# Batch 0's v is loaded beside k instead of behind q, and the first stage of a fused attention and MLP kernel is put in a new order

## The chip, the core and the metric

One Trainium2 chip, one of its cores. The metric is the device time of one execution, in microseconds (us), as the median of several runs. The engines are named as in the profile: PE (TensorE, with PEld for its weight loads), DVE (VectorE), ACT (ScalarE), POOL (GpSimd) and SP (SyncE). SP, ACT and POOL also issue DMAs; the transfers that SP issues show in the profile as queue q1, those that POOL issues as q0, those of ACT as q10.

## What is computed

```python
# per batch (8) and head (8): q, k, v are 576 x 64
q_s = exp(q - q.max(-1)) / sum over the 64 features
k_s = exp(k - k.max(tokens)) / sum over the 576 tokens
kv  = k_s^T v                              # 64 x 64 per head
x   = q_s kv, heads side by side           # 576 x 512 per batch
xn  = (x - mean) / sqrt(var + 1e-6) * g    # over the 512 columns
out = x + relu(xn w1) w2                   # w1: 512 x 2048, w2: 2048 x 512
```

Inputs and the output are fp32. The kernel multiplies in bf16.

## The kernel before

**Work as a whole.** Tokens 0 to 511 of a batch are one piece of work: four tiles of 128 tokens. The last 64 tokens of all eight batches make a ninth piece. For each piece the kernel forms x, normalises it, and runs the two MLP products on PE. The MLP products fill PE from about 15 us to the end. `run(main, side)` interleaves the two kinds of work by hand: `main` is the list of MLP steps, each with a weight, and `side` is a list of (position, function) that are issued when the running sum of the weights has reached the position. So the order on every engine is fixed when the kernel is built (`manual_schedule`), and each engine works through its list in order.

**Batch 0 is special.** Nothing can hide its attention, so `first_batch` writes that part out instruction by instruction. Its 576 tokens of k and v lie in 96 partitions with six tokens each (`T0 = 6`), in four pairs of heads (j = 0 to 3).

The loads are issued in this order. SP: q of tiles 0 and 1 (`load_q0(0, 2, nc.sync)`), then k in four pieces, one per head pair. ACT: the rows of g, 2 KB. POOL: first a small copy into a tile called `gate` (L1004), which reads a piece of q's tile; since POOL works in order, everything behind it waits until q's tiles 0 and 1 have landed. Behind it POOL issues v in three pieces (heads 0 to 3, 4 and 5, 6 and 7; L1006), q of tiles 2 and 3 (L970), the first 512 columns of w1 in two halves (L1013; by rows 0 to 255 and 256 to 511), the other three blocks of w1 (L99), and then w2 and the next batches.

The computation of batch 0 then goes like this:

- `exp_qt(0, t)` (ACT, L220) and `norm_q` (DVE: L229, L274, L923) make tile t of the softmax of q; `eq_pT` transposes it on PE (L928) and copies it to SBUF (L934 on DVE, L930 on ACT).
- `exp_k0(j)` (ACT, L293) is exp of k for head pair j. `z0_mm(j)` (PE, L306, 6 matmuls with one column) sums it over the tokens. `recip_z` (DVE, L314) inverts the sums, once for all four pairs. `kv0_mm(j)` multiplies exp(k) by v (PE, L321, 6 matmuls), scales the result on DVE (L322) into `kv_sb`, and spreads its negative row mean into `mbc` (L327 on ACT for j < 3, L331 on DVE for j = 3).
- `xT_mm(j, kh)` (PE, L342) forms, for tiles 0 and 1 and half kh of the columns, x transposed and with its mean already taken off. All four j add into one bank, so the bank is complete only after j = 3. `xT_out(i)` (L351 on DVE for i = 0 and 1, L353 on ACT for i = 2 and 3) scales column block i by g and writes it to `xnT`, the operand of the first MLP product.
- Tiles 2 and 3 go another way, inside the MLP steps: `q0_rest(t)` (PE: `zs` L940 and `po` L414), `x_fast` and `x_normed` (DVE: L464, L475), then `xn_pT` (PE L928, DVE L932).
- `warm(n)` issues n matmuls (L867) on a tile of zeros whose result nobody reads.

**The first MLP product** of batch 0 is `ph` (PE, L520). Its first eight matmuls need `xnT` of i = 0 and 1 and the first half of the first w1 columns; the next eight need i = 2 and 3 and the second half. After these come the matmuls for tile 2, then those that use the second block of w1 columns, and so on.

Of the kernel before, what the change touches and what calls it, by code (L numbers as in the profile page):

```python
# [12 lines left out]
FP32 = mybir.dt.float32  # L13
BF16 = mybir.dt.bfloat16
AF = mybir.ActivationFunctionType
# [5 lines left out]
def kernel(  # L21
# [16 lines left out]
    nc = tc.nc  # L38
# [4 lines left out]
    P = 128  # L43
# [3 lines left out]
    KO1 = DM // P  # L47
    KO2 = DH // P
    NP = H // 2
# [6 lines left out]
    T0 = 6  # L56
    P0 = S // T0
# [16 lines left out]
    gate = const.tile([P, 4], FP32)  # L74
# [42 lines left out]
    raws = {}  # L117
# [99 lines left out]
    def exp_qt(b, t):  # L217
        if t == 0 and b:
            new_eq(b)
        nc.scalar.activation(eqs[b][0][:, t], raws[b][2][:, :, t], AF.Exp)  # L220
# [68 lines left out]
    def exp_k0(j):  # L289
        hs = slice(2 * j, 2 * j + 2)  # L290
        if j == 0:
            eks[0] = raw.tile([P, T0, H, D], BF16, tag="kt", name="ek0", bufs=1)
        nc.scalar.activation(  # L293
            eks[0][0:P0, :, hs, :].rearrange("p t h d -> p h t d"), raws[0][0][0:P0, hs], AF.Exp
        )

    def k0_mm(j, t):
        hs = slice(2 * j, 2 * j + 2)
        return eks[0][0:P0, t, hs, :], raws["v0"][0:P0, hs, t, :], P

    def z0_mm(j):

        if j == 0:
            kvbox["z0"] = mm_ps.tile([P, NP], FP32, tag="m", name="z0")
        for t in range(T0):
            nc.tensor.matmul(  # L306
                kvbox["z0"][:, j : j + 1], k0_mm(j, t)[0], ones[0:P0],
                start=(j == 0 and t == 0), stop=(t == T0 - 1), skip_group_check=True,
            )

    def recip_z():
        kvbox["rz"] = sml.tile([P, NP], FP32, tag="rzk", name="rzk")
        kvbox["sum"] = sml.tile([P, NP], FP32, tag="lnv", name="kvs")
        nc.vector.reciprocal(kvbox["rz"], kvbox["z0"])  # L314

    def kv0_mm(j):
        pool, tag = (att_ps, "a") if j < 2 else (mm_ps, "m")
        pkv = pool.tile([P, P], FP32, tag=tag, name="pkv")
        for t in range(T0):
            lhsT, rhs, w = k0_mm(j, t)  # L320
            nc.tensor.matmul(pkv[:, 0:w], lhsT, rhs, start=(t == 0), stop=(t == T0 - 1))  # L321
        nc.vector.scalar_tensor_tensor(  # L322
            kv_sb[:, 0, j, :], in0=pkv, scalar=kvbox["rz"][:, j : j + 1], in1=diag,
            op0=ALU.mult, op1=ALU.mult, accum_out=kvbox["sum"][:, j : j + 1],
        )
        if j < NP - 1:
            nc.scalar.activation(  # L327
                mbc[:, j], ones_w, AF.Copy, scale=kvbox["sum"][:, j : j + 1]
            )
        else:  # L330
            nc.vector.tensor_scalar_mul(  # L331
                out=mbc[:, j], in0=ones_w, scalar1=kvbox["sum"][:, j : j + 1]
            )

    def xT_mm(j, kh):

        if j == 0:
            pobox["T", kh] = mm_ps.tile([P, 2, 2, P], FP32, tag="m", name="pxT")
        ops = [(kv_sb[:, 0, j, :], j % 2)] if j // 2 == kh else []
        ops += [(mbc[:, j], i) for i in range(2)]  # L340
        for n, (lhsT, i) in enumerate(ops):
            nc.tensor.matmul(  # L342
                pobox["T", kh][:, i], lhsT, eqTs[0][:, 0:2, j, :],
                start=(j == 0 and n == 0), stop=(j == NP - 1 and n >= len(ops) - 2),
                skip_group_check=True,
            )

    def xT_out(i):
        dst, src = xnTs[0][:, 0:2, i, :], pobox["T", i // 2][:, i % 2]
        if i < 2:  # L350
            nc.vector.tensor_scalar_mul(out=dst, in0=src, scalar1=g_one[:, i : i + 1])  # L351
        else:
            nc.scalar.activation(dst, src, AF.Copy, scale=g_one[:, i : i + 1])  # L353
# [509 lines left out]
    def warm(n):  # L863

        w = mm_ps.tile([P, 4, P], FP32, tag="m", name="warm")
        for _ in range(n):
            nc.tensor.matmul(w, junk, junk[:, 0:4].to_broadcast([P, 4, P]), start=True, stop=True)  # L867
# [77 lines left out]
    def eq_pT(c, t, eng):  # L945
        pe_T(eqTs[c], eqs[c][0][:, t].rearrange("p h d -> p (h d)"), t, eng)
# [4 lines left out]
    def g_columns():  # L951
        gcp = mm_ps.tile([P, KO1], FP32, tag="m", name="gcp")
        nc.tensor.matmul(gcp, raws["g"], ident_f, start=True, stop=True)
        nc.vector.tensor_copy(out=g_one, in_=gcp)
        nc.vector.tensor_scalar_mul(out=g_col, in0=gcp, scalar1=1.0 / DM)

    def first_batch():

        nc.scalar.preload_act_table_set("natural_log_exp_and_others")
        raws[0] = (  # L960
            mlp.tile([P, H, T0, D], FP32, tag="hT", name="kt0", bufs=1), None,
            raw.tile([P, H, T, D], FP32, tag="qt", name="qt"),
        )
        k0, _, q0 = raws[0]
        v0 = mlp.tile([P, H, T0, D], BF16, tag="hs", name="v0", bufs=1)
        raws["v0"] = v0

        def load_q0(t, tn, eng):
            ts = slice(t, t + tn)
            eng.dma_start(  # L970
                q0[:, :, ts],
                q[0, :, 0:SM, :].rearrange("h (p t) d -> p h t d", t=T)[:, :, ts],
            )

        def src0(x, h0, hn):
            return x[0, h0 : h0 + hn].rearrange("h (p t) d -> p h (t d)", t=T0)

        load_q0(0, 2, nc.sync)
        for h0 in range(0, H, 2):
            nc.sync.dma_start(  # L980
                k0[0:P0, h0 : h0 + 2].rearrange("p h t d -> p h (t d)"), src0(k, h0, 2)
            )
        raws["g"] = outp.tile([KO1, P], FP32, tag="ot", name="g_rows")
        nc.scalar.dma_start(
            raws["g"], bass.AP(moe_g_ln.tensor, moe_g_ln.offset, [[P, KO1], [1, P]])
        )
        nc.vector.memset(junk, 0.0)
        nc.vector.memset(eps_ln, 1e-6)
        nc.vector.memset(ones, 1.0)
        nc.vector.memset(bones, 0.0)  # L990
        nc.vector.memset(bones[0:64, 0:1], 1.0)
        nc.vector.memset(bones[64:P, 1:2], 1.0)
        nc.vector.memset(ones_w, -1.0 / DM)
        nc.vector.memset(diag, 0.0)
        for ps in halves:
            nc.vector.memset(diag[ps, ps], 1.0)
        nc.vector.memset(kv_sb[:, 1:B], 0.0)
        nc.vector.memset(vr, 0.0)
        for half in range(2):
            nc.vector.memset(vr[64 * half : 64 * half + 64, :, 4 * half : 4 * half + 4, D:], 1.0)  # L1000
        nc.vector.memset(vm[:, :, :, :, D:], 1.0)
        make_identity(nc, ident)
        nc.gpsimd.tensor_copy(out=ident_f, in_=ident[0:KO1, 0:KO1])
        nc.gpsimd.tensor_copy(out=gate, in_=q0[:, 1, 0, 0:4])  # L1004
        for h0, hn in ((0, 4), (4, 2), (6, 2)):
            nc.gpsimd.dma_start(  # L1006
                v0[0:P0, h0 : h0 + hn].rearrange("p h t d -> p h (t d)"), src0(v, h0, hn)
            )
        for t in range(2, T):
            load_q0(t, 1, nc.gpsimd)  # L1010
        for kh in range(2):
            ks = slice(2 * kh, 2 * kh + 2)
            nc.gpsimd.dma_start(w1_sb[:, ks, 0:512], w1_src[:, ks, 0:512])  # L1013
        for nb in range(1, 4):
            load_w1(nb)
        load_w2(0)
        load_w2(1)

        new_eq(0)
        start_x(0)  # L1020
        warm(17)
        for t in range(2):
            exp_qt(0, t)
            norm_q(0, t)
        eq_pT(0, 0, nc.vector)
        warm(6)
        eq_pT(0, 1, nc.vector)
        for j in range(NP):
            exp_k0(j)
            z0_mm(j)  # L1030
            if j == NP - 2:
                g_columns()
        recip_z()
        kv0_mm(0)
        kv0_mm(1)
        kv0_mm(2)
        xT_mm(0, 0)
        kv0_mm(3)
        exp_qt(0, 2)
        exp_qt(0, 3)  # L1040
        xT_mm(1, 0)
        xT_mm(2, 0)
        xT_mm(0, 1)
        xT_mm(3, 0)
        xT_out(0)
        xT_out(1)
        eq_pT(0, 2, nc.scalar)
        xT_mm(1, 1)
        xT_mm(2, 1)
        eq_pT(0, 3, nc.vector)  # L1050
        xT_mm(3, 1)
        xT_out(2)
        xT_out(3)

    def q0_rest(t):
        z_q(0, t)
        for i in range(NP):
            po_mm(0, t, i)
# [33 lines left out]
    with tc.manual_schedule(  # L1092
# [11 lines left out]
        def po_x(c, t):  # L1104
            for i in range(NP):
# [4 lines left out]
            mlp_steps(0),  # L1110
            [
                (2, lambda: (q0_rest(2), x_fast(0, 2), x_normed(2))),
                (4, lambda: q0_rest(3)),
                (6, lambda: (xn_pT(0, 2, nc.vector), x_fast(0, 3), x_normed(3))),
                (8, lambda: [po_mm(0, t, i) for t in range(2) for i in range(NP)]),
                (12, lambda: xn_pT(0, 3, nc.vector)),
# [74 lines left out]
```

## Time and profile before

| what | value |
|---|---|
| median of 3 runs | 262.32 us (262.25 to 262.44) |
| profiled execution, its own time | 262.09 us |
| its span (first to last instruction) | 260.3 us |
| granted PE clock over the span | 1.00 |
| busy: PE, DVE, ACT, POOL | 98%, 86%, 68%, 40% |
| time until PE's first `ph` matmul | 14.62 us |
| PE busy in the stretch 65 to 258 us | 191.26 of 193.00 us |

A row of the timeline reads: start, length, engine, line, operation, what it writes and what it reads, shape, number of instructions, and in brackets the idle time before it with what ended the wait. A row of the chain reads: start, length, what ran. In the rows of a DMA queue the numbers are packets, megabytes (as written at the destination) and the busy share of 16 engines, which passes 100% where packets overlap.

### The profile page before, as it was taken

The page shows a single profiled execution, that of the slowest core. Times are in us where ns is not written, and L with a number is a line of the kernel's source. Part 1 is how long each engine was busy: PE and PEld are TensorE (multiplying, and loading weights), DVE is VectorE, ACT ScalarE, POOL GpSimd, SP SyncE. Part 2 cuts the span into 40 slices and gives each one's busy share as a digit, 9 for nine tenths or more (in the row PEclk, how much of TensorE's full clock was granted, in tenths as well). Part 3 has the DMA queues.
Part 4 walks back from the last instruction along what each step waited for, and adds up shares of the span by engine and source line. Part 5 has one row for each costly group of instructions (what it writes and reads, how often), then busy time and mean ns, then how long its engine had stood idle before and what let it go on. Part 6 is the DMA issues. An engine that isn't in the chain of part 4 may idle for free.

```text
span 260.3 us, 7286 instructions
## 1 busy us (share of the span) xinstructions
PE 253.9 (98%) x2885; PEld 215.6 (83%) x2885; DVE 223.1 (86%) x542; ACT 177.5 (68%) x348; POOL 103.2 (40%) x160
## 2 busy tenths in 40 slices
PE   8899999999999999999999999999999999999993
PEld 3689755788888888888888988888889888888883
DVE  6768996989989998899889988998899889957873
ACT  4747790997988685888588858885788386647400
POOL 3953247410299409800980098008200900190000
PEclk9999999999999999999999999999999999999999
DMA  6999999988699995999699859989902630422014
GB/s 198 257 203 208 354 221 332 257 169 308 118 122 321 268 120 107 300 247 107 142 300 235 86 135 304 232 89 161 279 0 50 142 137 1 77 71 99 3 40 121
DMA packets 82618, 45.04 MB, mean 173 GB/s; under 512 B 58196, under 2 KB 79192, under 8 KB 82584
## 3 DMA queue, kind: packets, MB, share of 16 engines
q0 software_dynamic: 32464, 21.76, 45.8%
q1 hardware_dynamic: 49488, 22.29, 36.8%
q10 hardware_dynamic: 632, 0.53, 0.7%
q8 instruction: 22, 0.36, 0.6%
q14 instruction: 12, 0.10, 0.1%
HBM read 36.70 MB, written 9.44 MB: 177 GB/s over the span
## 4 chain that ended last, share of the span: by engine, by line
PE 92%; DMA 4%; POOL 2%; DVE 0%; issue 0%
PE ba L604 21%; PE bx L762 20%; PE bb L762 10%; PE ph L520 8%; PE bb L604 6%; PE be L604 5%; PE bc L604 5%; PE pc L556 5%; PE bc L762 5%; DMA w_raw<-in_moe_w_ch_dram 3%; PE pkv L371 2%; DMA qt<-in_q_dram 2%; PE po L403 2%; PE ptr L928 1%; PE po L414 1%; POOL v L1006 1%
## 5 line engine op out<-in xcount | busy, mean ns | idle before, releaser
L604 PEld LDWEIGHTS <-hs 128*128 128x128 bf16 x512 | 49.6, 98 | 6.0
L269 POOL TENSOR_TENSOR tq<-xnT 128x256 bf16<-128x256 bf16 x30 | 20.1, 671 | 85.3 <-PE bc L604 73.9
L762 PEld LDWEIGHTS <-w_raw 128*128 128x128 bf16 x480 | 46.7, 98 | 5.5
L604 PEld LDWEIGHTS <-hT 128*128 128x128 bf16 x392 | 37.6, 98 | 4.2
L762 PEld LDWEIGHTS <-w1g 128*128 128x128 bf16 x360 | 34.7, 98 | 4.3 <-issue 0.2
L762 PE MATMUL bx<-tq,w_raw 128*128 128x256 bf16 x240 | 31.3, 273 | 0.0
L604 PE MATMUL ba<-w_q,hs 128*128 128x256 bf16 x256 | 30.6, 273 | 0.0
L786 ACT COPY bc<-bx 128x512 f32<-128x512 f32 x30 | 16.7, 596 | 19.1 <-PE bx L762 19.1
L427 ACT ACTIVATE scrap<-x,mv 128x512 bf16<-128x512 bf16 x32 | 23.1, 723 | 4.6 <-DVE mv L457 4.4
L793 DVE TENSOR_TENSOR bb<-bx,s 128x512 f32<-128x512 f32 x30 | 19.5, 694 | 7.2 <-ACT s L790 4.5
L804 ACT ACTIVATE hT<-bb 128x512 bf16<-128x512 f32 x30 | 16.3, 595 | 9.3 <-PE bb L762 9.3
L804 ACT ACTIVATE hT<-bc 128x512 bf16<-128x512 f32 x30 | 16.5, 595 | 8.5 <-PE bc L762 8.5
L796 DVE TENSOR_TENSOR hT<-bx,s 128x512 bf16<-128x512 f32 x30 | 19.3, 684 | 3.2 <-PE bx L762 3.1
L587 DVE TENSOR_TENSOR hs<-hT 128x1024 bf16<-128x1024 bf16 x32 | 21.4, 672 | 0.5 <-ACT hT L804 0.5
L229 DVE TENSOR_REDUCE zq<-eq 128x16 f32<-128x1024 bf16 (+1 forms) x20 | 20.7, 1049 | 0.5 <-ACT eq L220 0.5
L269 POOL TENSOR_TENSOR tq<-xnT,tq 128x256 bf16<-128x256 bf16 x30 | 20.0, 669 | 1.1
L449 DVE SCALAR_TENSOR_TENSOR x<-po,rq 128x256 bf16<-128x256 f32 x48 | 17.5, 420 | 1.7 <-PE po L403 1.7
L790 ACT COPY s<-bb 128x512 f32<-128x512 f32 x30 | 16.6, 622 | 0.0
L804 ACT ACTIVATE hT<-bx 128x512 bf16<-128x512 f32 x30 | 16.4, 610 | 0.0
L762 PE MATMUL bx<-xnT,w1g 128*128 128x256 bf16 x120 | 16.2, 273 | 0.0
L762 PE MATMUL bx<-tq,w1g 128*128 128x256 bf16 x120 | 15.9, 272 | 0.0
L762 PE MATMUL bc<-xnT,w1g 128*128 128x256 bf16 x120 | 15.8, 273 | 0.0
(157 smaller groups left out, 535.0 us busy)
## 6 DMA issues: line engine op xcount, KB each, us to landing
out_dram<-ot POOLq DMA_DIRECT2D x30, 256.0 KB, 4.4
kt<-in_k_dram SPq DMA_DIRECT2D x5, 1024.0 KB, 11.6
qt<-in_q_dram SPq DMA_DIRECT2D x4, 1024.0 KB, 9.9
qt<-in_q_dram POOLq DMA_DIRECT2D x2, 1024.0 KB, 12.7
kt<-in_k_dram POOLq DMA_DIRECT2D x2, 1024.0 KB, 14.5
vm<-in_v_dram POOLq DMA_DIRECT2D x16, 128.0 KB, 12.4
qt<-in_q_dram SPq DMA_DIRECT2D x3, 512.0 KB, 5.7
w_raw<-in_moe_w_ch_dram POOLq DMA_DIRECT2D x3, 512.0 KB, 10.5
```

Source lines behind the costliest of these rows:

```text
L229: nc.vector.reduce_sum(eqs[c][1][:, ts], eqs[c][0][:, ts], axis=AX.X)
L269: nc.gpsimd.tensor_tensor(out=dst[:, t], in0=x[:, t], in1=y[:, t], op=ALU.subtract)
L427: nc.scalar.activation(scrap, x[:, t], AF.Square, bias=mv[:, t, 0:1], scale=-float(DM), accum_out=mv[:, t, 1:2],)
L449: nc.vector.scalar_tensor_tensor(x[:, t].rearrange("p (i two d) -> p i two d", two=2, d=D)[:, :, half], in0=pobox[c, t][half], scalar=1.0, ...
L520: nc.tensor.matmul(ph[:, m % 2, at : at + tn], (w1g if c else w1_sb)[:, ko, m * P : (m + 1) * P], xnTs[c][:, t0 : t0 + tn, ko, :], start=( ...
L587: nc.vector.tensor_tensor(out=dst, in0=x, in1=y, op=op)
L604: nc.tensor.matmul(hbox[bank][:, t, cs], lhsT, rhs[:, cs], start=first and (own or t == 0) and k == 0, stop=k == KH - 1, skip_group_check= ...
L762: nc.tensor.matmul(dst[:, q], lhsT, rhs, start=first and q == 0 and ko == 0, stop=ko == 1, skip_group_check=True)
L786: nc.scalar.copy(at[g, "c"], at[g, "x"])
L793: nc.vector.tensor_tensor(out=at[g, "b"], in0=at[g, "x"], in1=at[g, "s"], op=ALU.add)
L796: nc.vector.tensor_tensor(out=h_out(g, 1, 1), in0=at[g, "x"], in1=at[g, "s"], op=ALU.add)
L804: nc.scalar.activation(h_out(g, odd, half), at[g, name], AF.Relu)
```

## The change

- `gate` is now copied from the rows of g (L1005 of the changed kernel), so v and all that POOL issues behind it wait for these 2 KB and no longer for q's tiles 0 and 1.
- `z0`, its inversion and the scaling are set by halves: `recip_z(0)` for pairs 0 and 1, `recip_z(1)` for 2 and 3, with a bank of two columns each. `kv0_mm` keeps the matmuls; the scaling is a step of its own, `kv0_out(j, eng)`, with `mbc` on DVE for j = 0 and 3 and on ACT for j = 1 and 2.
- The written-out order becomes: pairs 0 and 1 up to their `kv0_mm`, the transposes of q's tile 1, g's columns, then pair 2 and pair 3, with `xT_mm` of a pair for both halves kh one behind the other.
- `xT_out` goes to DVE for i = 0 and 2 and to ACT for i = 1 and 3. In the built program ACT's step for i = 1 carries a semaphore wait for DVE's step for i = 0, and that for i = 3 one for i = 2.
- ACT's exp for tiles 2 and 3 stands between these; tile 2's transposes stand at the end of `first_batch`, now copied by DVE; those of tile 3 stand at position 3 of the MLP steps, copied by ACT, and `q0_rest(3)` moves from position 4 to 5.
- The six `warm` matmuls in the middle become three groups of two at other places.

```diff
     def z0_mm(j):
-        if j == 0:
-            kvbox["z0"] = mm_ps.tile([P, NP], FP32, tag="m", name="z0")
+        half, at = divmod(j, 2)
+        if at == 0:
+            kvbox["z0", half] = mm_ps.tile([P, 2], FP32, tag="m", name="z0")
...
-    def recip_z():
+    def recip_z(half):
+        if half == 0:
+            kvbox["rz"] = sml.tile([P, NP], FP32, tag="rzk", name="rzk")
+            kvbox["sum"] = sml.tile([P, NP], FP32, tag="lnv", name="kvs")
+        nc.vector.reciprocal(kvbox["rz"][:, 2 * half : 2 * half + 2], kvbox["z0", half])
...
+    def kv0_out(j, eng):
         nc.vector.scalar_tensor_tensor(
-            kv_sb[:, 0, j, :], in0=pkv, scalar=kvbox["rz"][:, j : j + 1], in1=diag,
+            kv_sb[:, 0, j, :], in0=kvbox["kv0", j], scalar=kvbox["rz"][:, j : j + 1], in1=diag,
             op0=ALU.mult, op1=ALU.mult, accum_out=kvbox["sum"][:, j : j + 1],
         )
-        if j < NP - 1:
+        total = kvbox["sum"][:, j : j + 1]
+        if eng is nc.scalar:
             nc.scalar.activation(mbc[:, j], ones_w, AF.Copy, scale=total)
         else:
             nc.vector.tensor_scalar_mul(out=mbc[:, j], in0=ones_w, scalar1=total)
...
     def xT_out(i):
-        if i < 2:
+        if i % 2 == 0:
             nc.vector.tensor_scalar_mul(out=dst, in0=src, scalar1=g_one[:, i : i + 1])
...
-        nc.gpsimd.tensor_copy(out=gate, in_=q0[:, 1, 0, 0:4])
+        nc.gpsimd.tensor_copy(out=gate[0:KO1], in_=raws["g"][:, 0:4])
...
         eq_pT(0, 0, nc.vector)
-        warm(6)
-        eq_pT(0, 1, nc.vector)
-        for j in range(NP):
+        for j in range(2):
             exp_k0(j)
             z0_mm(j)
-            if j == NP - 2:
-                g_columns()
-        recip_z()
-        kv0_mm(0)
-        kv0_mm(1)
+        recip_z(0)
+        warm(2)
+        for j in range(2):
+            kv0_mm(j)
+        eq_pT(0, 1, nc.vector)
+        g_columns()
+        kv0_out(0, nc.vector)
+        exp_k0(2)
+        z0_mm(2)
+        exp_k0(3)
+        kv0_out(1, nc.scalar)
+        warm(2)
         kv0_mm(2)
         xT_mm(0, 0)
+        xT_mm(0, 1)
+        z0_mm(3)
+        recip_z(1)
         kv0_mm(3)
+        kv0_out(2, nc.scalar)
+        kv0_out(3, nc.vector)
+        xT_mm(1, 0)
+        xT_mm(1, 1)
         exp_qt(0, 2)
-        exp_qt(0, 3)
-        xT_mm(1, 0)
         xT_mm(2, 0)
-        xT_mm(0, 1)
         xT_mm(3, 0)
         xT_out(0)
         xT_out(1)
-        eq_pT(0, 2, nc.scalar)
-        xT_mm(1, 1)
         xT_mm(2, 1)
-        eq_pT(0, 3, nc.vector)
         xT_mm(3, 1)
+        exp_qt(0, 3)
         xT_out(2)
         xT_out(3)
+        eq_pT(0, 2, nc.vector)
+        warm(2)
...
                 (2, lambda: (q0_rest(2), x_fast(0, 2), x_normed(2))),
-                (4, lambda: q0_rest(3)),
+                (3, lambda: eq_pT(0, 3, nc.scalar)),
+                (5, lambda: q0_rest(3)),
```

## The prediction

> **What bounds the kernel now.** I read the page's chain first, to see which engine carries the end.
>
> ```profile
> PE 92%; DMA 4%; POOL 2%; DVE 0%; issue 0%
> ```
>
> PE carries it; DMA and POOL come in only at the start. So I asked for the chain up to 22 us:
>
> ```profile
> 0.74 4.29 DMA qt<-in_q_dram
> ...
> 5.08 0.19 POOL gate L1004
> 5.27 2.07 POOL v L1006 x3
> ...
> 9.82 6.86 DMA w_raw<-in_moe_w_ch_dram
> 16.68 0.05 issue
> 16.72 0.61 PE ph L520 x4
> ```
>
> Up to 16.68 us the chain is loads in one line: q lands, POOL passes its gate, issues v and w1, and the second half of w1's first columns lands at 16.68. After 16.72 PE has no wait of a tenth of a us or more except one near 19.3 us (0.11, on DVE's xn). So whatever moves the second-column block of `ph` (it starts at 19.57) moves the end by as much. Later loads leave room: the next w1 block lands at 10.53 + 8.7 = 19.2 us.
>
> The timeline shows the stage that the change rewrites:
>
> ```profile
> 7.13 0.84 ACT L293 ACTIVATE ek<-kt 96x768 bf16<-96x768 f32 x1 [0.20 <-DMA kt<-in_k_dram]
> 8.16 1.82 ACT L293 ACTIVATE ek<-kt 96x768 bf16<-96x768 f32 x2 [0.19 <-DMA kt<-in_k_dram]
> ...
> 10.22 1.26 PE L321 MATMUL pkv<-v,ek 96*128 96x128 bf16 x18
> ...
> 14.62 0.60 PE L520 MATMUL ph<-xnT,w_raw 128*128 128x256 bf16 x4
> ...
> 16.72 0.61 PE L520 MATMUL ph<-xnT,w_raw 128*128 128x256 bf16 x4 [0.41 <-DMA w_raw<-in_moe_w_ch_dram]
> ```
>
> exp of k follows k's landings one by one (about 7.1, 8.1, 9.1 us). v's first piece, issued at 5.20 and 5.0 us under way, lands at 10.2, and PE's first `pkv` starts there, 4.40 us before the first `ph`. PE then still waits for w1: the first stage has 0.41 us to spare.
>
> The DMA queues in two windows, 5.0 to 7.5 and 7.5 to 8.4 us:
>
> ```profile
> q1 hardware_dynamic: 509, 0.72, 107.7%
> ```
>
> ```profile
> q0 software_dynamic: 117, 0.09, 64.1%
> q1 hardware_dynamic: 98, 0.13, 55.3%
> ```
>
> k alone keeps the engines full. v's packets begin at 7.5, 2.3 us after their issue, as k runs out, and the two share the time. There is no idle DMA time after 2.7 us that an earlier v could fill.
>
> **The change, part by part.** *Gate.* g's 2 KB are moved by 2.1 us (q10's eight packets all lie in the window 1.5 to 2.7). POOL's copy took 0.19, so v is issued near 2.2 instead of 5.20. With v's own delay of 2.3 us its packets begin at about 4.5; with that of an output store on an idle queue (issued 128.41, first packet 129.6: 1.2 us) at 3.4; if they wait for k to run out, at 7.5. I take 4.5, v's own row, and keep both ends. All POOL issues behind v come earlier too, but w1's bytes stand behind the same bytes of q, k and v. With the engines full, w1's landings stay (16.7, 19.2), and so do those of q's tiles 2 and 3 (12.4 and 13.2, where ACT's exps of them start); ACT asks for them at 13.8 and later. What is queued behind the new waits: on ACT, which works in order, a late exp of k holds back the other exps and `mbc`; on PE, `z0` of a late pair holds back all that stands behind it.
>
> *What v takes from k.* k costs 0.72 MB / 1536 B = 470 packets in 2.5 us, 5.3 ns each. v costs 3.8 ns (window 8.4 to 11.0: 698 packets, nearly all v, in 2.6 us). In turns of one packet each, a piece of k (192 packets) takes 192 x 9.1 ns = 1.75 us instead of 1.02. From 4.5 us on, k's pieces then land at 6.5, 8.3, 10.0 and 11.3 (before 6.1, 7.1, 8.1, 9.1) and v's at 8.6, 10.3 and 11.7 (before 10.2, 10.9, 11.7). The Trainium skill (DMA: Bandwidth & Descriptors, "Issuing engines are not separate DMA queues") says that DMAs started by different engines run on the same 16 DMA engines and interleave, so that issuing from several saves only sequencer time. It speaks against this change, and the two windows agree. By it the sum stays as it is; only a rate above both rows would alter it.
>
> *The order behind the first `pkv`.* Let X be the start of the first `pkv`. Before, X = 10.22 and the first `ph` is at X + 4.40. In the new order PE has, from X: two `kv0_mm` 0.67 (12 x 0.056), tile 1's transposes 0.22, g's columns 0.30, `z0_mm(2)` 0.15, two warm matmuls 0.43, `kv0_mm(2)` 0.33, five `xT_mm` matmuls 0.55 with 0.07 of waiting for `mbc`: X + 2.73. Then the last pair's chain: `z0_mm(3)` and its latency 0.32, reciprocal 0.04 + 0.18, scalings of pairs 2 and 3 0.04 + 0.34 + 0.36, `mbc` 0.04 + 0.25, two `xT_mm` to their end 0.45: X + 4.75. DVE's eviction 0.04 + 0.48 and then ACT's, which waits for it, 0.04 + 0.47: X + 5.8. PE meanwhile runs six `xT_mm` (0.65), tile 2's transposes and two warm matmuls (0.65), and reaches the first `ph` at X + 5.9. The stage is 1.5 us longer from X, because the transposes of tile 1, g's columns, half of z0 and four warm matmuls, which stood in the wait for v before, now stand behind it; and the two evictions of a bank are one behind the other (0.99 us; before, 0.88 for two on DVE). The gate has to bring X forward by 1.5 us, to 8.7, only to break even.
>
> *X itself.* X is the later of v's first landing + 0.06, and the second piece of k + 0.04 + 0.84 (exp) + 0.06 + 0.15 (z0) + 0.43 (warm). With the landings above: 8.6 and 8.3 + 1.52 = 9.8. First `ph`: 15.7.
>
> *From the first `ph` to the block that started at 19.57.* Before: 4.95 us, with 0.41 of waiting for w1 in it. New: w1 is there (PE asks for its second half at 17.1), but tile 3's transposes (0.22) stand there, and `zs` of tile 3 then waits about 0.4 for ACT's copy (0.57). DVE's chain for tile 3 (L943, L932, L464, L475) starts later by that too. It adds to 4.98.
>
> *Sum.* 15.7 + 4.98 - 19.57 = +1.1. On the profiled execution's own 262.09 (260.3 of span and 1.8 around it) that is 263.2; the median of the runs stands 0.23 higher, so 263.4. As the bounds of v's start and of the shared rates lean to a smaller cost (v starting at 5.2 gives X = 9.3 and +0.6), I forecast 263.3. Nothing else costs: the reciprocal in two parts adds one 0.18 on DVE while it waits for PE, and `mbc` of pair 0 on DVE 0.25 instead of 0.40.
>
> **Rivals.** *v still starts only when k runs out* (7.5 us), so the load does not move. For: no q0 packet before 7.5, though issued at 5.2. Against: an output store needs only 1.2 us. Then X = 10.24 and `ph` at 16.1: +1.5, 263.8. Chance 0.18.
>
> *v starts at 3.4, while q's tiles are still moving.* q then lands near 5.5 instead of 5.0, k's second piece at 9.1, X = 10.6: +1.9, 264.2. Against: 0.79 MB moved from 2.7 to 5.0, so q is nearly through by then. Chance 0.13.
>
> *Not slower: k and v together move faster than either alone.* For: k ran at 289 GB/s in 5.0 to 7.5 while the queue moved 343 from 2.7 to 5.0. k's second piece at 7.2, v's first at 8.6 and w1 0.7 us earlier need one us saved before 8.7. This decides: with X at 8.63, its floor by exp of k's second piece, `ph` comes at 14.53 and the kernel gains 0.06: 262.3. Earlier v gains nothing more. Against: in 7.5 to 8.4 the shares of both sum to the usual 119%. Chance 0.14, and 0.06 for a gain beyond it that I have not found.
>
> *PE's clock.* The first warm matmuls stand 0.43 us apart and the late ones about 0.2. With more waiting between 8 and 12 us the slow spacing could return: up to +1 on top. The Trainium skill (TensorE: Matmul & The Clock Gate, "The HAM clock gate") has the slow clock come back after an idle window of about 3.4 us; by that it stays away here, as PE's longest wait would be 1.4 us. Chance 0.04.
>
> **How the numbers follow.** The forecast's case, v starting between 4.2 and 6 us with turns of one packet, has 0.45: +0.6 to +1.3, 262.9 to 263.6. The likeliest value in it is 263.3. The range takes in the faster mixing below (262.3, less 0.1 for the spread of the runs) and q's delay above (264.2, with 0.2 for the clock): 262.2 to 264.4, leaving out under 2 in 10. A measurement of this kernel can tell about 0.2%, 0.52 us, from no change. Faster by that: 0.06. Within: most of the mixing case and a little of the forecast's low end, 0.18. Slower: 0.76.
>
> **What would show it.** Right: v issued near 2.2, ACT's exps of k later than before by about 1 us at the second and 2 at the last, the first `pkv` between 9.3 and 10, 5.9 us to the first `ph`, no PE wait for w1, and then the same chain of PE. Wrong: a first `ph` before 14.6, w1's second half landing before 16, k's exps unchanged beside an early v, or a PE wait that is neither of these.

## The result, and the profile after

The changed kernel takes 264.74 us (median of 6 runs, 264.23 to 265.51) against 262.40 (262.25 to 262.55): 2.34 us longer, a ratio of 1.0092 [1.0070, 1.0115]. The forecast was +1.0 and a range that ended at 264.4. The runs lie in two groups of three: 264.23 to 264.29 with a mean granted TensorE clock of 0.999 to 1.0, and 265.19 to 265.51 with 0.990 to 0.994. The profile of the kernel before had 1.00. The profiled execution is one of the slower three (265.19, span 263.4).

The page's chain, shares by engine, and then the first pieces of the chain in order of time (start, length, what; a piece begins here where the one before it ends, so that the first `ph` reads 17.62, and 17.46 in the timeline below):

```profile
PE 94%; DMA 4%; ACT 0%; issue 0%; DVE 0%; POOL 0%
```

```profile
2.19 0.12 POOL gate L1005
2.32 7.96 DMA v<-in_v_dram
10.28 0.04 issue
10.32 0.83 PE pkv L323 x12
...
17.62 0.44 PE ph L521 x4
```

The gate opened as forecast, and v was issued at 2.32 instead of 5.20. But its first piece took 7.96 us and landed at 10.28, against 10.18 before. Three microseconds of earlier issue bought nothing. The chain no longer runs over w1; from v's landing on it is PE.

The DMA queues from 5.0 to 7.5 us, and then from 7.5 to 8.4 (packets, MB, share of 16 engines):

```profile
q1 hardware_dynamic: 391, 0.55, 84.7%
q0 software_dynamic: 134, 0.10, 26.6%
```

```profile
q0 software_dynamic: 111, 0.09, 60.2%
q1 hardware_dynamic: 103, 0.16, 58.7%
```

Both windows are as full as before (111% and 119%; before 108% and 119%). What v gets, k loses: v's first packet comes at 6.16 (before: 7.72), and k's last two pairs land at 8.48 and 10.08 instead of 8.14 and 9.12. ACT's exps follow them:

```profile
8.50 0.84 ACT L293 ACTIVATE ek<-kt 96x768 bf16<-96x768 f32 x1 [0.46 <-DMA kt<-in_k_dram]
10.10 0.84 ACT L293 ACTIVATE ek<-kt 96x768 bf16<-96x768 f32 x1 [0.76 <-DMA kt<-in_k_dram]
```

PE's timeline at the three points that the prediction set, first `pkv`, first `ph`, and the block of `ph` with second columns (before: 10.22, 14.62, 19.57):

```profile
10.32 0.83 PE L323 MATMUL pkv<-v,ek 96*128 96x128 bf16 x12 [1.47 <-DMA v<-in_v_dram]
...
17.46 0.60 PE L521 MATMUL ph<-xnT,w_raw 128*128 128x256 bf16 x4
...
22.46 1.80 PE L521 MATMUL ph<-xnT,w_raw 128*128 128x256 bf16 x15
```

From first `pkv` to first `ph` it is 7.14 us, not the 5.9 worked out. The stage is read by stretches of a microsecond (busy share and count of PE, PEld, DVE, ACT, POOL; then granted clock, DMA share, GB/s):

```profile
12.00:13.00 1.00, 1.00 (x10) 0.78 (x9) 0.78 (x5) 0.12 (x1) 1.00 (x3) 0.67 1.15 214
13.00:14.00 1.00, 1.00 (x12) 0.75 (x11) 0.00 (x0) 0.28 (x1) 1.00 (x2) 0.50 1.22 201
14.00:15.00 1.00, 1.00 (x13) 0.89 (x11) 0.69 (x4) 0.23 (x1) 0.43 (x1) 0.50 1.26 207
15.00:16.00 1.00, 1.00 (x8) 0.77 (x6) 0.45 (x3) 0.69 (x2) 0.64 (x1) 0.62 1.24 207
```

The clock falls to half. If it is either 1 or 0.5, the four shares make 3.4 us of half speed, from about 12.3 to 15.8, begun two microseconds after the end of a 1.47 us wait for v.

At full clock the executions (264.23 to 264.29) lie inside the range; the fallen clock of the other half puts the median outside. So two things were to be settled: what makes the way longer at full clock, and what makes the clock fall.

### The profile page after: what moved, and what is told of

Its sections match the earlier page's. It is cut to its first block, busy times and chain, and to the rows that moved or that the text cites. A ratio compares the mean times of both kernels' runs of the same rounds, so it can differ in the third digit from the quotient of the medians.

```text
span 263.4 us, 7282 instructions
## 1 busy us (share of the span) xinstructions
PE 255.9 (97%) x2882; PEld 216.8 (82%) x2885; DVE 222.8 (85%) x544; ACT 177.0 (67%) x347; POOL 103.4 (39%) x160
## 4 chain that ended last, share of the span: by engine, by line
PE 94%; DMA 4%; ACT 0%; issue 0%; DVE 0%; POOL 0%
PE ba L605 21%; PE bx L763 20%; PE bb L763 10%; PE ph L521 8%; PE bb L605 6%; PE be L605 5%; PE bc L605 5%; PE pc L557 5%; PE bc L763 5%; DMA v<-in_v_dram 3%; PE pkv L372 2%; PE po L404 2%; PE pxT L343 1%; PE ptr L929 1%; PE po L415 1%; PE pkv L323 1%
## 5 line engine op out<-in xcount | busy, mean ns | idle before, releaser
L787 ACT COPY bc<-bx 128x512 f32<-128x512 f32 x30 | 16.7, 597 | 19.1 <-PE bx L763 19.1
L763 PE MATMUL bc<-xnT,w1g 128*128 128x256 bf16 x120 | 15.8, 273 | 0.0
```

Source lines behind the costliest of these rows:

```text
L763: nc.tensor.matmul(dst[:, q], lhsT, rhs, start=first and q == 0 and ko == 0, stop=ko == 1, skip_group_check=True)
L787: nc.scalar.copy(at[g, "c"], at[g, "x"])
```

## Experiments: the gate or the order

Two kernels each take one half of the change. Runs are split below by the mean granted clock of each execution, at 0.9955, since a fall shows there. Of 107 runs of the kernel before that stand beside these experiments, 8 lie under it. The ratios and their intervals are taken from the record; they need not equal the quotient of the two medians, least of all where the executions fall into groups.

**The gate alone** (the kernel before, with the new gate):

```
-        nc.gpsimd.tensor_copy(out=gate, in_=q0[:, 1, 0, 0:4])
+        nc.gpsimd.tensor_copy(out=gate[0:KO1], in_=raws["g"][:, 0:4])
```

> The kernel before with only the gate changed: POOL's gate copies from g_rows, the order on every engine is the old one. Theory (the loss lies in the new order, v's landing hardly moves because the DMA engines are full either way): first pkv stays near 10.2 to 10.3, the first ph follows 4.4 to 4.9 us later since k's pairs land up to 1 us later (10.1 for the last, against 9.1 before), and the time is 0.3 to 0.8 us over the kernel before, 262.7 to 263.2. Rival (the early v is what costs: contention with q and k): 1.5 us or more over the kernel before, 263.9 or above. Rival (v early pays): first pkv before 9.8 and a time below 262.2.

Measured: 263.94 us beside 262.31, ratio 1.0030 [1.0005, 1.0055]. The five executions at full clock have a median of 262.79, so +0.5; the seven below it 264.14. The price at full clock is what the theory said, the way to it is not: k's last pair landed at 10.40, `z0` waited 1.12 us for its exp, and the first `pkv` came at 11.49 instead of 10.2. The profiled execution is one with a fallen clock, so how the 1.3 us of delay shrink to 0.5 at full clock was not traced; in this profile w1's second half lands 0.8 us earlier (15.86), and the wait of 0.41 us for it is gone.

**The order alone** (the changed kernel with the old gate, the edit above reversed):

> The changed kernel with the old gate (POOL copies from q0), so v's loads are issued near 5.2 as before, and only the order is new. Theory: loads as in the kernel before (k 6.1/7.1/8.1/9.1, v 10.2/10.9/11.7), first pkv near 10.2, the first ph 5.9 us later at full clock; the time is 1.3 to 1.9 us over the kernel before, 263.7 to 264.3, and 1.2 us more (264.9 to 265.5) in executions in which the clock granted to TensorE falls near 12 to 16 us. Rival (the contention of the early gate is the loss): at most 0.8 us over the kernel before.

Measured: 266.13 us, ratio 1.0116 [1.0079, 1.0152]. At full clock (3 of 10) the median is 263.80, +1.5; the other seven, 264.56 to 267.42. The loads land as before (v 10.22, k's last pair 9.11). Most of the loss at full clock is therefore in the order; an early v is not needed for it. Not foreseen: four of the seven lie above 266.4, at a clock of 0.984 and 0.985, where one fall gives 0.990 to 0.994.

## Experiments: the clock

**Fill the wait** (8 warming products for 2 ahead of the first `pkv`):

```
         recip_z(0)
-        warm(2)
+        warm(8)
         for j in range(2):
             kv0_mm(j)
```

> The changed kernel with 8 in place of 2 warming products ahead of the first pkv: they fill about 1.3 of the 1.47 us for which TensorE waits for v, and delay nothing, since v is what ends that wait. Theory (the fall of the clock to 0.50 near 12 to 16 us comes of that wait): granted clock 1.0 throughout in every execution, first ph about 5.9 us after the first pkv, all runs in one group at 264.1 to 264.4, median ratio to the kernel before near 1.007. Rival (the fall has another source, such as light matrix work from 12 us on): the clock falls again in some executions and the runs lie in two groups 1 us apart.

Measured: 264.01 us, ratio 1.0056 [1.0037, 1.0074], all 12 executions at 0.996 or more. Later variants of this kernel are compared with it. The same stretches as above:

```profile
12.00:13.00 1.00, 1.00 (x20) 0.95 (x18) 0.46 (x3) 0.40 (x1) 1.00 (x2) 1.00 1.18 217
13.00:14.00 1.00, 0.96 (x14) 0.64 (x10) 0.83 (x6) 0.31 (x1) 1.00 (x2) 1.00 1.25 205
```

First `pkv` 9.98, first `ph` 15.91: 5.93 us, the 5.9 of the prediction. Six products that compute nothing cost nothing here, since they stand in a wait (v landed at 9.94), and the clock stays up.

**The changed kernel again**, unedited:

> The changed kernel itself, once more, on the chip of this call. Theory (the fall of the clock behind TensorE's wait for v decides between two groups): executions at 264.0 to 264.6 with a granted clock of 0.996 or more, others at 265.1 to 265.8 with 0.99 to 0.995, neither group empty; the run with 8 warming products, which differs in six products alone, had no execution below 0.996 in 12.

Measured: 264.77 us, ratio 1.0114 [1.0069, 1.0159]. Three executions lie at 264.10 to 264.25 (0.999 to 1.0), one at 265.30 (0.994), two at 266.70 and 267.00 (0.984). Two groups were expected; there is a third. The profiled one is at full clock and serves as the pair to the profile above.

**The wait without the change** (the kernel before, its 6 warming products taken out):

```
         eq_pT(0, 0, nc.vector)
-        warm(6)
         eq_pT(0, 1, nc.vector)
```

> The kernel before without its 6 warming products (1.31 us on TensorE between 7.65 and 8.98): TensorE then waits about 1.3 us for DVE's tile 1 in the middle of light work, with nothing else changed, no load among it. Theory (a wait of 1 us or more amid light work is what makes the clock fall, whatever is waited for): the clock falls to 0.50 for some 3.4 us in a good part of the executions, whose time is 0.6 to 1.5 us over the others. Rival (the fall belongs to the changed loads or to the new order): no execution below 0.995 beyond the few that the kernel before has, and the time within 0.3 us of it.

Measured: 263.02 us, ratio 1.0024 [0.9997, 1.0051]; 7 of 12 executions lie under 0.9955, at 262.99 to 265.00, the five others at 262.09 to 262.98. The time is not told from that of the kernel before; the falls are, as 3 of the 28 runs of the kernel before beside it fell. Its profile, PE's timeline and then the stretches:

```profile
9.03 0.40 PE L928 MATMUL ptr<-ident,eq 128*128 128x128 bf16 x4 [1.03 <-DVE eq L923]
```

```profile
10.00:11.00 1.00, 0.77 (x12) 0.63 (x12) 0.41 (x3) 0.23 (x1) 1.00 (x2) 0.68 1.31 233
11.00:12.00 1.00, 1.00 (x12) 1.00 (x11) 0.36 (x2) 0.07 (x1) 1.00 (x2) 0.50 1.15 372
...
17.00:18.00 1.00, 1.00 (x12) 0.87 (x10) 0.34 (x1) 0.04 (x2) 0.53 (x1) 0.90 1.25 207
```

With half speed in every stretch between, this is 6.8 us, twice the 3.4: that is what a mean of 0.984 to 0.987 is. No load and no order was changed here, so the fall belongs to the gap in matrix work. The Trainium skill (TensorE: Matmul & The Clock Gate, "The HAM clock gate") has a window of about 3.4 us that runs freely, whatever the kernel does, and the slow clock after an idle one. The 3.4 and 6.8 us agree with the window. That it must be idle does not: gaps of 1.0 to 1.5 us were enough, in some executions.

Which executions fall has to do with where the windows lie. The clock steps on a grid that begins where it first rises; there the spacing of the first warming products halves, from 0.43 to 0.22 us. In the profile of the changed kernel it rises at 5.52, falls at 12.35 and is back at 15.76: two windows of 3.41, then one. With the gate alone the first two times are 5.17 and 12.00, here 6.95 and 10.37. Each time the window that ends at the fall holds nearly all of the wait: 1.39 of 1.47 us, all of the 1.12, all of the 1.03. In the changed kernel's repeat, at full clock, the grid begins at 5.94, and its edge at 9.35 cuts the same wait into 0.54 and 0.94. This is read from four profiles, not tested; the order alone, with 1.12 us of its wait in one window and no fall, shows that it is not all.

Over all kernels of this study the count of executions under 0.9955 follows PE's longest wait between 8 and 12 us in the profile: with 1.5 us it is 13 of 22 (the changed kernel, the order alone); with 1.0 to 1.1 us, 14 of 24 (the gate alone, before without warming); with 0.8 us, 3 of 18; with 0.5 to 0.6 us, 2 of 24; with less, 0 of 73. The kernel before, which has no such wait either, fell in its 8 of 107, so this is not the whole rule. The count leaves out waits that end before 8 us, right behind the 17 warming products at the start: the kernel before has one of 0.99 us there, up to 7.42, and a kernel without a fall in 6 executions one of 1.14. So the length of a wait alone does not decide.

## Experiments: what the order costs at full clock

All of these start from the kernel with 8 warming products (264.01, ratio 1.0056).

**The two later groups of warming products taken out:**

> As the run with 8 warming products ahead of the first pkv, and the two later groups of 2 taken out (0.43 us each on TensorE by their places in the profile of the changed kernel). Theory: the clock stays at 1.0 (it is the wait that mattered), and the first ph comes 0.4 to 0.9 us earlier than with them, 263.3 to 263.9. Rival (those groups stand where TensorE waits anyway): no difference from the run with them, 264.1 to 264.4. Rival (they are needed for the clock): the clock falls, 265 and above.

Measured: 264.08 us, ratio 1.0062 [1.0042, 1.0083], 0 of 12 under 0.9955. The 0.86 us of PE time that they take gained nothing: from first `pkv` to the block it is 10.85 us, against 10.93. PE waits instead for `mbc`, `xnT` and tile 3's `eqT`.

**x's eviction as before** (`if i < 2` for `if i % 2 == 0`):

> The run with 8 warming products with the eviction of x as before: columns 0 and 1 (one PSUM tile) on DVE, 2 and 3 on ACT. Theory (in the changed kernel's trace ACT's eviction of the second column of a PSUM tile starts only when DVE's of the first has ended, so the split over two engines brings no overlap): the same time within 0.3 us, 263.7 to 264.3. Rival (the split does shorten the way to the first ph): 0.4 us or more slower, 264.4 or above.

Measured: 264.15 us, ratio 1.0067 [1.0054, 1.0081]: the same. The split over two engines changes nothing.

**The last tile's steps as before:**

```
+        exp_qt(0, 3)                      # behind exp_qt(0, 2)
...
-        exp_qt(0, 3)                      # ahead of xT_out(2)
         eq_pT(0, 2, nc.vector)
+        eq_pT(0, 3, nc.scalar)
...
-                (3, lambda: eq_pT(0, 3, nc.scalar)),
-                (5, lambda: q0_rest(3)),
+                (4, lambda: q0_rest(3)),
```

> The run with 8 warming products with the last tile's steps as before: exp_qt(0, 3) and eq_pT(0, 3) ahead of the first ph, q0_rest(3) at 4 among the MLP's products. Theory (the moved transposes only changed places on TensorE, which has no time to spare there): first ph about 0.2 us later, no wait of 0.24 us for eqT behind it, the block of ph with second columns within 0.3 us of where it was, 263.7 to 264.3. Rival (moving them behind the MLP products gained): 264.4 or above; rival (it lost): 263.5 or below.

Measured: 263.91 us, ratio 1.0054 [1.0041, 1.0068]: the same. The wait of 0.24 us goes, the transposes come in its place.

What is left is what stands between the first `pkv` and its eviction. DVE's timeline in the changed kernel:

```profile
11.41 0.42 DVE L935 COPY eqT<-ptr 128x512 bf16<-128x512 bf16 x1 [2.07 <-PE ptr L929]
11.76 0.15 DVE L955 COPY g_one<-gcp 128x4 f32<-128x4 f32 x1
11.82 0.15 DVE L956 TENSOR_SCALAR g_col<-gcp 128x4 f32<-128x4 f32 x1
11.89 0.34 DVE L326 SCALAR_TENSOR_TENSOR kv_sb<-pkv,rzk,diag 128x128 bf16<-128x128 f32 x1
```

Tile 1's transposes and g's columns need nothing of v. They wait for it all the same, because PE works in order and they are queued behind `pkv`; and DVE, which works in order too, can only then do their copies, ahead of the eviction of `pkv`.

**These steps ahead of the first `pkv`:**

```
         recip_z(0)
-        warm(8)
+        eq_pT(0, 1, nc.vector)
+        g_columns()
+        warm(6)
         for j in range(2):
             kv0_mm(j)
-        eq_pT(0, 1, nc.vector)
-        g_columns()
```

> The run with 8 warming products ahead of the first pkv, changed in one place: the transposes of q's tile 1 (eq_pT(0, 1)) and g_columns stand ahead of the first pkv, in the time in which TensorE waits for v, and 6 warming products fill the rest of it. Theory (what makes the new order longer is that these steps are queued behind the first pkv, so that DVE's eqT copy of 0.42 us and the two g copies come between pkv and its eviction: in the run with 8 the first kv_sb eviction starts 1.58 us after the first pkv): that eviction starts near 0.5 us after the first pkv, the block of ph with second columns comes about 1 us earlier, 262.9 to 263.3. Rival (v's later pieces, landing 0.7 and 1.5 us behind the first, set the pace of the chain): a gain below 0.3 us, 263.7 to 264.1.

Measured: 263.82 us, ratio 1.0053 [1.0040, 1.0066]. The time is not the theory's but lies in the rival's range, 263.7 to 264.1. That does not decide, since the 6 warming products hold the first `pkv` until 10.96, 0.9 us after v's landing. The eviction came 0.54 us behind `pkv` as expected. The next run takes the products out.

**The same with 2 warming products:**

> The run with q's tile 1 and the g columns ahead of the first pkv, with 2 instead of 6 warming products between: in that run the 6 ended 0.94 us after v's first piece had landed and so delayed the first pkv to 10.96. Theory (from first pkv to the block of ph with second columns takes 10.3 us with those steps ahead, against 10.9 with them behind): first pkv near 10.1, block near 20.4, time 262.9 to 263.3. Rival (the chain is paced by v's later pieces): block at 20.8 or later, 263.5 or above.

Measured: 263.23 us beside 262.66, ratio 1.0023 [1.0001, 1.0044], under the 1.0056 of the kernel with 8. DVE's timeline:

```profile
9.43 0.42 DVE L935 COPY eqT<-ptr 128x512 bf16<-128x512 bf16 x1
...
11.32 0.35 DVE L326 SCALAR_TENSOR_TENSOR kv_sb<-pkv,rzk,diag 128x128 bf16<-128x128 f32 x1 [1.33 <-PE pkv L323]
```

The time is the one forecast. In the profiled execution, one of the slowest of the twelve, v landed late, at 10.74; from first `pkv` to the block it is 10.27 us instead of 10.93. Two thirds of a microsecond are these steps.

## Experiments: the loads

**k's pairs 2 and 3 behind v's first piece**, on POOL's queue (`load_k0` is the load of one pair, made a function):

```
-        for h0 in range(0, H, 2):        # SP: k's four pairs
+        for h0 in (0, 2):                # SP: pairs 0 and 1
...
                 v0[0:P0, h0 : h0 + hn].rearrange("p h t d -> p h (t d)"), src0(v, h0, hn)
             )
+            if h0 == 0:
+                load_k0(4, nc.gpsimd)
+                load_k0(6, nc.gpsimd)
```

> The run with 8 warming products, with k's head pairs 2 and 3 issued on POOL behind v's first piece, in place of SP: the first piece of v then competes with q and k's first two pairs only. Theory (v landed no sooner in the changed kernel because k's bytes were ahead of it or beside it): v's first piece lands near 8.3, the first pkv starts at 8.8 to 9.2 (k's pair 1 and its exp end there), and since the chain of the new order is the same from there, the time is 1.0 to 1.4 us below the run with 8 warming products: 262.6 to 263.1. Rival (the later pairs of k and v or q's tiles take over the end of the chain): the first pkv comes earlier by about 1 us and the time by less than 0.4 us.

Measured: 264.07 us, ratio 1.0060 [1.0047, 1.0074]. v's first piece landed at 8.52, 1.7 us sooner, but the 8 products held PE until 9.82, so this run says little of the loads.

**The same with 2 warming products:**

> The run with k's pairs 2 and 3 queued behind v's first piece, with 2 in place of 8 warming products ahead of the first pkv: in that run v's first piece landed at 8.52 but the 8 products held TensorE until 9.82. Theory of the change (an earlier v shortens the way by as much): first pkv near 8.6, block of ph with second columns 10.9 us later, 19.5, time 262.2 to 262.5. Rival, which I now hold likelier (the last pieces end the chain: k's pair 3 with its exp at 11.3, v's last piece at 11.7): first pkv near 8.6, the last pkv not before 12.0, block at 20.3 to 20.8, time 263.0 to 263.5.

Measured: 262.99 us, ratio 1.0013 [0.9995, 1.0031]. PE's timeline:

```profile
8.65 0.83 PE L323 MATMUL pkv<-v,ek 96*128 96x128 bf16 x12
...
10.95 0.50 PE L323 MATMUL pkv<-v,ek 96*128 96x128 bf16 x6
...
11.99 0.49 PE L323 MATMUL pkv<-v,ek 96*128 96x128 bf16 x6
...
19.98 3.24 PE L521 MATMUL ph<-xnT,w_raw 128*128 128x256 bf16 x36
```

The rival came nearer: the first `pkv` is 1.57 us earlier than before, the last one 0.16 later (before: 11.83), and the median is at the rival's edge. The block lies between the two forecasts, in the fastest of the twelve executions. What v's first piece gained (it landed at 8.41), k's later pairs lost: they landed at 9.43 and 10.49 (before: 8.14 and 9.12). PE waits for the exp of the first of them up to 10.35 and then runs without a gap to the last `pkv`, 0.26 us behind v's last piece, which landed at 11.73 as before (11.72). In the kernel before, too, the last `pkv` started 0.1 us behind v's last landing. An earlier first piece had next to nothing to win.

**A rival for v's late start** (DVE's 1.55 us memset of `kv_sb` moved behind `recip_z(0)`):

> The run with 8 warming products, with DVE's memset of kv_sb (1.55 us at 2.34) moved to DVE's wait for TensorE near 9.3. In the changed kernel v's first packets came 3.7 us after POOL's issue, against 2.3 in the kernel before. Theory (DVE's memset holds back POOL's writing of descriptors): v's first packets 0.7 us or more earlier, near 5.3 or before. Rival (they wait for the DMA engines, which are full with q's and k's packets): first packets near 6.0 as before. The time: within 0.3 us of the run with 8, as v's last piece lands when all bytes ahead of it are through.

Measured: 264.20 us beside 262.66, ratio 1.0042 [1.0019, 1.0066], the time of the kernel with 8. v was issued at 2.46, its first packet came at 6.47: no sooner. DVE's memset isn't what holds v back.

## Experiments: a version that uses this

The steps free of v ahead of `pkv`; `pkv(2)`, `z0(3)` and `pkv(3)` as their loads come, x's products around them; eviction and last tile as before; k's pairs 2 and 3 behind v's first piece. Its order:

```
        recip_z(0); warm(3); eq_pT(0, 1, nc.vector); g_columns()
        kv0_mm(0); kv0_mm(1); kv0_out(0, nc.vector)
        exp_k0(2); z0_mm(2); exp_k0(3); kv0_out(1, nc.vector)
        warm(1); kv0_mm(2); z0_mm(3); recip_z(1); xT_mm(0, 0); kv0_mm(3)
        kv0_out(2, nc.scalar); kv0_out(3, nc.vector)
        xT_mm(0, 1); exp_qt(0, 2); exp_qt(0, 3); xT_mm(1, 0); xT_mm(1, 1)
        xT_mm(2, 0); xT_mm(3, 0); xT_out(0); xT_out(1); eq_pT(0, 2, nc.scalar)
        xT_mm(2, 1); eq_pT(0, 3, nc.vector); xT_mm(3, 1); xT_out(2); xT_out(3)
```

> What the runs so far point to, put together: k's pairs 2 and 3 behind v's first piece, q's tile 1 and the g columns ahead of the first pkv, the eviction and the last tile's steps as in the kernel before, x's products by the last pkv as late as v's last piece lands. Theory: last pkv at 11.8 to 12.1, first ph at 14.4 to 14.8 (w1's first half lands at 14.4), its second half without the wait of 0.41 us that the kernel before has at 16.72, block of ph with second columns at 19.1 to 19.6: 261.9 to 262.4, faster than the kernel before by up to 0.4 us. Rival (in-order queues lose what the loads give): block at 20 or later, 262.8 or above.

Measured: 261.99 us beside 262.66, ratio 0.9963 [0.9941, 0.9985], 0 of 12 executions under 0.9955. Of all kernels here it is the one that is faster than the runs of the kernel before beside it, by 0.4%. PE's timeline:

```profile
9.64 0.84 PE L323 MATMUL pkv<-v,ek 96*128 96x128 bf16 x12
...
12.09 0.50 PE L323 MATMUL pkv<-v,ek 96*128 96x128 bf16 x6
...
14.73 0.60 PE L521 MATMUL ph<-xnT,w_raw 128*128 128x256 bf16 x4
...
19.32 3.90 PE L521 MATMUL ph<-xnT,w_raw 128*128 128x256 bf16 x42
```

The first `ph` is no earlier than before (14.62). The block is, by 0.25 us: w1's second half is there, and no wait is left.

**This order with the changed kernel's loads** (all of k on SP):

> The order of the version that beat the kernel before, with the changed kernel's loads (all of k on SP). Theory (what counts is that nothing that can run earlier is queued behind a load's wait, and that v's last piece, landing near 11.6 with either order of loads, ends the chain): last pkv at 11.9 to 12.2, first ph at 14.6 to 15.0, 262.0 to 262.6. Rival (the win came of k's pairs 2 and 3 standing behind v's first piece): last pkv near 12.8 or later, 262.9 or above.

**And with the loads of before** (old gate too):

> As that, with the gate on q as in the kernel before (v issued near 5.2): all loads as in the kernel before. Theory: k's pairs come up to 1 us sooner and v's as late as before, the last pkv at 11.8 to 12.2, 262.0 to 262.6, with a part of the executions about 1 us longer, where TensorE's wait for v from 9.7 on makes the clock fall. Rival (the early v is needed): 262.9 or above without a fall of the clock.

Measured: 262.12 us, ratio 1.0000 [0.9974, 1.0026], and 262.21, ratio 1.0005 [0.9969, 1.0040], beside 262.42. At full clock both have medians of 262.1 to 262.2, near the 261.99 above: the schedule of the loads hardly matters in this order. Beside the kernel before, though, these two are level with it, and the version above is ahead; whether its loads gain a few tenths at full clock is not told apart. Their PE waits 0.61 and 0.76 us for v, and 1 and 3 of 12 executions fell in clock; with k's later pairs behind v's first piece there is no such wait, and none fell. The rivals, which ask for an early v, fail at full clock.

From the first `pkv` to the block these two take 9.23 and 9.11 us; the kernel before took 9.35 (with its wait of 0.41), the changed kernel 11.15, with 8 products 10.93, and with the steps free of v ahead 10.27. So the order holds the whole loss at full clock. The last 1.0 us, from 10.27 to 9.23, went with the rest of the new order (x's products around `pkv`, `mbc` of pair 1, the later warming products, eviction, last tile). Which of these it is was not settled: single ones, taken out or put back above, gave nothing, but that was in the kernel with 8 products.

## Why the prediction was wrong in size

The direction and the rule (what moves the block moves the end) held: from block to end it is 240.7 us before and 240.9 in each profile of the changed kernel. The steps, against the changed kernel's profile at full clock (span 262.3, 2.0 over before):

- **v's start, the step that failed first.** "I take 4.5, v's own row" puts v's packets 2.3 us behind the issue. The first one came at 6.16, 3.8 us behind it (in the kernel before at 7.72, 2.5 behind). From there v's first piece took 4.1 us, as the turns with k had it (8.6 - 4.5), and landed at 10.28: the turns held, the start did not. So X = 10.29 instead of 9.8, and v sets it, not k's second piece, which landed at 7.17 and not at 8.3. k paid less than was worked out (pair 3 at 10.08, not 11.3), and v gained nothing of its 1.6 us. By the prediction's own turns a start at 6.16 gives a landing at 10.3 and +1.6; the "+1.3" that it wrote for a start at 6 was too little. What holds v back until 6.16 stays open; DVE's memset does not.
- **The rivals.** That in which "the load does not move", 263.8, has the X that was measured, for another reason: v did start before k ran out, at k's expense. The 264.2 of the rival with an early v is nearer still, by luck: q's tiles landed at 5.04, not 5.5.
- **X to first `ph`, 5.9 us.** Measured 6.16 at full clock, and 5.93 with 8 warming products. The 0.2 between them is one term, "`mbc` of pair 0 on DVE 0.25": 0.55 at full clock, 0.26 with 8 products, see below.
- **First `ph` to block, 4.98 us:** 4.99. The steps for tile 3 were right.
- **Block to end, nothing:** 0.13.
- Sum at full clock: 0.07 + 1.76 + 0.04 + 0.13 = 2.0, where the prediction had -0.42 + 1.5 + 0.03 = +1.1.
- **The clock, the step that put the median outside.** It was a rival with a chance of 0.04, set aside because PE's "longest wait would be 1.4 us" and the idle window that it cites from the Trainium skill is 3.4. The wait was 1.47 us, and the clock fell in 6 of 12 executions of the changed kernel, at a price of 0.98 us in the profiled one (7.14 against 6.16) and up to 2.8 in others (267.00 against 264.20). The prediction saw the wait and the mechanism, and trusted a rule. The 6 warming products that the change moves away had covered just such a gap: without them the kernel before fell in 7 of 12.
- **w1's landing, a sign of being wrong that came true.** Its second half landed at 15.62, not 16.7; the first `ph` came later than that by itself, so it decided nothing. The 16.68 of the kernel before, and with it the 0.41 us to spare, looks like an accident of that profile: there a packet of 16 KB of the instruction queue, 0.95 us long, began at 15.90 among w1's packets (`q8 instruction: 1, 0.02, 4.9%` in the window 15.5 to 16.7), in the changed kernel at 17.05, behind them. The last kernel above, with the loads of before, had w1 at 15.91. No run moves that packet alone.

## What to carry to other kernels

On in-order queues, look at what stands behind the instruction that waits for the load: whatever does not need it belongs ahead of it, on the engine that waits and on the ones fed by it. While the DMA engines are full, as here, an earlier issue gained only when bytes ahead of it were moved behind it, and then the last piece, not the first, said what there was to win. Filler products in a gap of matrix work are part of the path's time even when they lie on no path; before taking them out, price the clock.

## What the runs showed of the hardware

DVE's `mbc` (bf16 to bf16 in SBUF) takes 0.25 us in most places, and 0.34 to 0.78 in some where POOL is issuing a DMA. In the kernel with the order alone, DVE's line and then POOL's:

```profile
14.54 0.67 DVE L334 TENSOR_SCALAR mbc<-ones_w,kvs 128x128 bf16<-128x128 bf16 x1
```

```profile
14.18 1.02 POOL L130 DMA_DIRECT2D qt<-in_q_dram  x1
```

DVE's ends at 15.21 and POOL's at 15.20. In the changed kernel it was 0.54, ahead of everything that `x`'s products need of pair 0. An issue beside it is not enough, as the kernel with 8 products shows:

```profile
11.94 0.26 DVE L334 TENSOR_SCALAR mbc<-ones_w,kvs 128x128 bf16<-128x128 bf16 x1
```

```profile
11.81 1.49 POOL L103 DMA_DIRECT2D w_sb<-in_moe_w_ch_dram  x2
```

Here DVE began 0.13 us behind POOL, in the order alone 0.36, in the changed kernel 0.25. The Trainium skill (SBUF — State Buffer, "SBUF: two separate sides") has the two engines share a port pair, where DVE runs in a 2-port mode, as an exclusive lock, held for a whole instruction, so that the later one waits. The two ends agree with it; the 0.26 does not, unless POOL takes the lock only some way into its issue. No run takes POOL's issue away to test it.

The rest of the surprise is the clock above: half speed in units of 3.4 us after gaps of 1.0 to 1.5 us, in some executions.
